# Attention and a gated feed-forward layer in one kernel: the first two heads in blocks of four key tiles, and query projections spread over the run

## The chip, the cores and the metric

The kernel runs on one core of one Trainium2 chip. The metric is the device time of one execution in microseconds (us), lower being better. A core has a matrix engine (TensorE, called PE in the profile, with PEld for its weight loads), a vector engine (VectorE, DVE), a scalar engine (ScalarE, ACT), a general engine (GpSimd, POOL) and SyncE (SP), which here only issues transfers. Sixteen DMA engines do the transfers. Each engine runs its own instructions in the order in which the program lists them.

## The reference

The input x has 2048 rows (tokens) of 512 numbers. One set of keys and values of width 16 serves all 32 heads; the feed-forward layer is 1792 wide; a gate g per token mixes the two.

```python
q = (x @ wq).reshape(B, S, H, Dh).transpose(0, 2, 1, 3)      # 32 heads of 16
k = x @ wk;  v = x @ wv                                      # one head of 16
p = softmax(einsum("bhqd,bkd->bhqk", q, k) * Dh ** -0.5)
a = einsum("bhqk,bkd->bhqd", p, v) ... @ wo
b = (silu(x @ w_gate) * (x @ w_up)) @ w_down
g = sigmoid((x * gate_w).sum(-1))
return g * a + (1 - g) * b
```

## The kernel before

All of it is one program with an order written out by hand. Numbers that need more than one rounded factor are held as a high part and a low part, so that a product takes three matmuls (`three`, line 111): high by high, high by low, low by high.

**The opening (lines 501 to 652).** x arrives, is transposed on TensorE and split. Keys and values are projected (`project_kv`). Then the queries of the first eight heads (m = 0) are projected for the four chunks c of 512 tokens, and `fill(GAP)` (line 652) does three more query projections whole. There are sixteen query projections: m = 0 to 3 (eight heads each) by c = 0 to 3. `query(m, c)` (line 214) makes one of them as a job of 12 matmuls; its inner function `keep` (line 224) empties the PSUM bank into a high part `qh`, a low part `ql` and a bound `qb` (the absolute value times the largest key, from which a head's score limit is had), takes a maximum, and stores the three parts to `q_d` in DRAM. For m = 0, head 0's rows go straight from these buffers into its tile `QS[0]` (line 244, sixteen small transfers), and the twelve stores to `q_d` come after all four chunks (line 650). For the other heads `load_head(h)` (line 660) reads four pieces from `q_d`, 64 and 192 KB in turn.

**The heads (lines 673 to 720).** A head is sixteen key tiles of 128 keys. For a tile, `score` (line 673) makes two pieces, one per pair of query chunks: two matmuls that use 64 rows of the array each and run beside one another, into one of two PSUM buffers `pss`. `exps` (line 687) takes the exponential on ScalarE, or, for some pieces, half from PSUM and half later from SBUF, where VectorE has copied it meanwhile (the copy of line 684). `mix` (line 692) multiplies a whole tile by the values: 8 records of line 700. At a head's end the sum is copied out (line 718) and divided in six pieces of VectorE work (`LATER`), the last of which stores the head to `o_d`.

**The feed-forward work** fills TensorE between the scores. `JOBS` (line 376) lists it: nine query projections that are left over, then for each chunk c the gate and up projections of 14 slices in groups of 5, 5 and 4, and behind each group the four `down` jobs of the group before. `feed(n)` takes n steps; in a step two jobs advance, one on the array's lower 64 rows and one on its upper 64 (`Halves`, line 394). When a job ends, its PSUM bank is emptied by VectorE at once (`EVAC`), except where a copy of a score is due next (`HOLD`). Work that can wait goes to the list `DEFER`, with a cost in us and a budget of 3.8 per block. Three PSUM banks `pf` serve the jobs. Weights come through two buffers `wraw`, are split on GpSimd (lines 107 and 108, through `load_split`), and in later chunks come back from DRAM ready split.

**The order of the heads.** The first two heads (32 tiles) go through the loop of lines 794 to 815, `BEGIN` = 16 turns of two tiles: four score pieces, four exponentials, all on ScalarE, 8 steps of `feed`, then `settle()`, which empties `DEFER`, and the two mixes. From tile 32 on `block` (line 731) does four tiles at a time: 8 score pieces and 16 steps in the order of `STEPS`, three of the eight pieces split between ScalarE and VectorE (`KINDS`, `EXPS`), then the deferred work and four mixes. The first such block (`TURN`) has ten score pieces. A block makes the scores of two tiles beyond those that it mixes. After the last block the jobs that are left run whole (`whole`, line 380) and `finish` multiplies the heads by wo.

**Memory.** `PT` holds six finished tiles, three in `bp` and three in a pool that is opened once the last query projection is done (`open_acc`, line 264), for until then the split x of chunks 2 and 3 and the split wq lie there. `ACC` holds sums of the feed-forward output.

Of the kernel before, what the change touches and what calls it, by code (L numbers as in the profile page):

```python
# [18 lines left out]
P = 128  # L19
S = 2048  # L20
D = 512
# [25 lines left out]
PTB = 3  # L47
WRB = 2
BLOCK = 4
BEGIN = 16  # L50
STOP = 2
EARLY = 6
OUTS = (1, 2, 3, 0)
# [3 lines left out]
TURN = "SS" + "SFF" * 8  # L57
# [5 lines left out]
def tile_gated_mix(ctx, tc, x, wq, wk, wv, wo, w_gate, w_up, w_down, gate_w, out):  # L63
# [10 lines left out]
    q_d = dpool.tile([H, 3 * DH, S], F32, name="q_d")  # L74
# [19 lines left out]

    qpool = tc.alloc_tile_pool(name="qpool", bufs=1, side="right")
# [7 lines left out]
    ACC, PAIR = {}, []  # L103
# [19 lines left out]
    ACTS, DEFER, LOADS, HOLD, EVAC, FRESH = [], [], [], [], [], set()  # L123
# [5 lines left out]
    def settle():  # L129
        FRESH.clear()  # L130
        run(ACTS, len(ACTS))
        while DEFER:
            DEFER.pop(0)[2]()
# [75 lines left out]
    WQ, QS, STORES = {}, {}, []  # L209

    def load_wq(m):
        WQ[m] = load_split(wq_v[:, :, m * P:(m + 1) * P], f"wq{m}", 1, qpool)

    def query(m, c):
# [8 lines left out]

        def keep(ps):
            qh = wp.tile([P, CH], F32R, name="hh", bufs=7)
            ql = wp.tile([P, CH], F32R, name="hl", bufs=7)

            if m:
                qb = wp.tile([P, CH], F32, name="ht" if c % 2 else "hs", bufs=2)
                nc.vector.tensor_copy(qh, ps)  # L230
            else:
                qb = wp.tile([P, CH], F32R, name="hl" if c % 2 else "hh", bufs=7).bitcast(F32)
                nc.scalar.activation(qh, ps, AF.Copy)
                nc.scalar.activation(qb.bitcast(F32R), ps, AF.Abs, scale=kmax)
            nc.vector.tensor_tensor(ql, ps, qh.bitcast(F32), ALU.subtract)
            if m:
                nc.vector.tensor_scalar(qb, qh.bitcast(F32), kmax, None, op0=ALU.mult)
                nc.vector.scalar_tensor_tensor(qb.bitcast(F32R), qb, -1.0, qb, op0=ALU.mult, op1=ALU.max)
            parts = [ql, qh, qb.bitcast(F32R)]
            if not m:  # L240
                for h, qs in QS.items():
                    for i, part in enumerate([qh] + parts):
                        row = c % 2 * RT + i * DH
                        nc.sync.dma_start(qs[row:row + DH, c // 2, :].bitcast(F32), part[h * DH:(h + 1) * DH].bitcast(F32))

            def store():
                for j, part in enumerate(parts):
                    nc.sync.dma_start(q_d[m * HG:(m + 1) * HG, j * DH:(j + 1) * DH, cs], part.bitcast(F32))

            if m:  # L250
                store()
            else:
                STORES.append(store)
            nc.vector.tensor_reduce(top[:, t:t + 1], qb, axis=AX.X, op=ALU.max)

        return Job(3 * KD, lambda: m in WQ, terms, keep)

    def queries():
        jobs = [query(m, c) for m in range(1, KD) for c in range(NCH)]
        jobs[-1].after.append(open_acc)  # L260
        jobs[-1].after.append(lambda: nc.vector.tensor_reduce(top[:, KD * NCH:], top[:, :KD * NCH], axis=AX.X, op=ALU.max))
        return jobs

    def open_acc():
        qpool.release()
        for name in ("accp", "bp2"):
            PAIR.append(tc.alloc_tile_pool(name=name, bufs=3, side="right"))
# [60 lines left out]
    def down(ns, c, i):  # L328
# [11 lines left out]
        def add(ps):  # L340
            if c not in ACC:
                ACC[c] = PAIR[0].tile([P, TC, D], F32, name="acc")
# [11 lines left out]


    def jobs():
        late = []
        for m, c in enumerate(ORDER):
            for fs in GROUPS:
# [7 lines left out]
                for j, job in enumerate(new):  # L367
                    yield job
                    if late and j:
                        yield late.pop(0)  # L370
                yield from late
# [129 lines left out]
    with tc.tile_pool(name="apool", bufs=1) as ap, tc.tile_pool(name="apool2", bufs=2) as a2:  # L501
# [29 lines left out]
        sel_i = ap.tile([P, HG], I32, name="sel_i")  # L531
        nc.gpsimd.iota(sel_i, pattern=[[-DH, HG]], base=0, channel_multiplier=1)
        sel_a = ap.tile([P, HG], F32, name="sel_a")
# [416 lines left out]
```

## Time and profile before

| | |
|---|---|
| median of three runs | 1343.21 us (1341.99 to 1344.04) |
| the profiled execution's own time | 1340.92 us |
| its span, first to last instruction | 1339.1 us |
| TensorE, busy | 1327.4 us, 99% |
| ScalarE, busy | 1069.0 us, 80% |
| VectorE, busy | 710.3 us, 53% |
| GpSimd, busy | 220.3 us, 16% |
| DMA, all queues | 151.84 MB |

The times of the table's lower part are of one profiled execution. A busy TensorE says little by itself, since its matmuls overlap: what counts is from one start to the next. A row of the view in order of time has the start, the length, the engine with the line, what is written and read, and how many instructions were merged; in brackets is the engine's idle time before it and what ended it. SPq rows are transfers as SyncE issues them; their length is the issue, not the transfer. In a table by windows a row has the stretch, its length, each engine's busy time with its count, the clock granted to TensorE as a share of full speed, the DMA engines' busy share and GB/s.

### The profile page before, as it was taken

Reading aid. Unit: us, or ns where it says so; the run is one execution under the profiler, and the core shown is the slowest. Engines: PE = TensorE matmul, PEld = TensorE weight load, DVE = VectorE, ACT = ScalarE, POOL = GpSimd, SP = SyncE. Lnnn points to the kernel's source line nnn. Section 1 sums busy time; section 2 is a strip of 40 time slices with the busy share of each in tenths; the row PEclk is TensorE's granted clock in tenths of the full one; section 3 lists DMA queues with packets and bytes.
Section 4 is the critical chain, followed back from the end, with each engine's and each line's share of the span. In section 5 each row is a group of like instructions: output and inputs, shape, how many; then the busy total and the mean of one; then the engine's idle time right before and its main releaser. Section 6 shows DMA issues by size and latency. Waiting matters only on the chain.

```text
span 1339.1 us, 26770 instructions
## 1 busy us (share of the span) xinstructions
PE 1327.4 (99%) x10743; PEld 769.7 (57%) x10743; DVE 710.3 (53%) x1221; ACT 1069.0 (80%) x1475; POOL 220.3 (16%) x228
## 2 busy tenths in 40 slices
PE   9999999999999999999999999999999999999998
PEld 7655555555555555555555555555555555555586
DVE  4555565465455555555555555455445565455442
ACT  4578888888888888888888888888888888888511
POOL 5141321152042141143020000000000000001223
PEclk9999999999999999999999999999999999999999
DMA  8455221131135372275162342243132342333154
GB/s 278 137 178 191 67 60 36 36 105 46 54 106 156 117 232 68 68 212 159 38 206 85 127 131 84 68 133 97 52 99 68 126 147 68 99 108 115 53 184 144
DMA packets 104178, 151.84 MB, mean 113 GB/s; under 512 B 12657, under 2 KB 43633, under 8 KB 102385
## 3 DMA queue, kind: packets, MB, share of 16 engines
q1 hardware_dynamic: 102320, 149.86, 36.4%
q8 instruction: 88, 1.44, 0.5%
q10 hardware_dynamic: 1728, 0.20, 0.1%
q14 instruction: 42, 0.34, 0.1%
HBM read 98.11 MB, written 51.38 MB: 112 GB/s over the span
## 4 chain that ended last, share of the span: by engine, by line
PE 98%; DVE 1%; ACT 1%; issue 0%; POOL 0%; DVEq 0%; ACTq 0%
PE pf L192 38%; PE po L700 34%; PE pss L680 21%; PE pf L117 4%; ACT pt L688 0%; PE pss L562 0%; PE po L549 0%; DVE xl L567 0%; PE pss L602 0%; DVE acc L345 0%; DVE hs L282 0%; POOL wul L108 0%; DVE wkv_l L108 0%; ACT xh L566 0%; DVE ot L464 0%
## 5 line engine op out<-in xcount | busy, mean ns | idle before, releaser
L688 ACT ACTIVATE pt<-pss 128x1024 f32<-128x1024 f32 (+1 forms) x1024 | 842.0, 876 | 177.7 <-PE pss L680 146.5
L684 DVE COPY pt<-pss 128x512 f32<-128x512 f32 x354 | 244.8, 691 | 421.4 <-PE pss L680 386.5
L700 PE MATMUL po<-pt,vaug 128*32 128x512 f32 x4096 | 467.6, 595 | 0.0
L680 PE MATMUL pss<-qs,ks 64*128 64x512 f32 x2048 | 402.4, 417 | 1.2 <-ACT pt L688 1.1
L680 PEld LDWEIGHTS pss<-qs,ks 64*128 64x128 f32 x2048 | 193.1, 184 | 218.7 <-ACT pt L688 183.5
L700 PEld LDWEIGHTS po<-pt,vaug 128*32 128x32 f32 x4096 | 119.2, 109 | 260.3 <-issue 255.2
L688 ACT ACTIVATE pt<-pt 128x512 f32<-128x512 f32 x354 | 195.7, 620 | 0.0
L192 PE MATMUL pf<-xh,wgl 64*128 64x512 f32 (+1 forms) x440 | 162.0, 391 | 0.0
L192 PE MATMUL pf<-xh,wgh 64*128 64x512 f32 (+1 forms) x440 | 160.8, 392 | 0.3
L192 PE MATMUL pf<-xl,wgh 64*128 64x512 f32 (+1 forms) x440 | 160.3, 390 | 0.0
L192 PE MATMUL pf<-xh,wuh 64*128 64x512 f32 (+1 forms) x440 | 158.3, 392 | 1.0 <-POOL wuh L107 0.5
L192 PE MATMUL pf<-xl,wuh 64*128 64x512 f32 (+1 forms) x440 | 158.1, 390 | 0.0
L192 PE MATMUL pf<-xh,wul 64*128 64x512 f32 (+1 forms) x440 | 157.1, 391 | 0.4 <-POOL wul L108 0.4
L192 PE MATMUL pf<-wdh,hl 64*128 64x512 f32 (+1 forms) x427 | 143.8, 390 | 0.0
L192 PE MATMUL pf<-wdh,hh 64*128 64x512 f32 (+1 forms) x427 | 143.3, 390 | 0.0
L192 PE MATMUL pf<-wdl,hh 64*128 64x512 f32 (+1 forms) x427 | 143.3, 390 | 0.0
L709 DVE RECIPROCAL rsb<-rsb 128x128 f32<-128x128 f32 x128 | 117.0, 935 | 10.1 <-issue 7.8
L447 POOL CAST xh<-wraw 128x512 fp32r<-128x512 f32 x4 | 2.9, 729 | 536.8 <-DMA wraw<-o_d 536.8
L192 PEld LDWEIGHTS pf<-xh,wgh 64*128 64x128 f32 (+1 forms) x440 | 78.5, 185 | 9.6 <-issue 1.3
L192 PEld LDWEIGHTS pf<-xh,wuh 64*128 64x128 f32 (+1 forms) x440 | 77.2, 185 | 9.7 <-issue 1.9
L192 PEld LDWEIGHTS pf<-xl,wgh 64*128 64x128 f32 (+1 forms) x440 | 78.5, 185 | 5.8
L192 PEld LDWEIGHTS pf<-xh,wgl 64*128 64x128 f32 (+1 forms) x440 | 78.5, 185 | 5.4
(158 smaller groups left out, 1361.5 us busy)
## 6 DMA issues: line engine op xcount, KB each, us to landing
qs<-q_d SPq DMA_DIRECT2D x62, 192.0 KB
wraw<-in_B_w_gate_dram SPq DMA_DIRECT2D x28, 256.0 KB
wraw<-in_B_w_up_dram SPq DMA_DIRECT2D x28, 256.0 KB
wraw<-in_B_w_down_dram SPq DMA_DIRECT2D x28, 256.0 KB
wgh<-w_d SPq DMA_DIRECT2D x28, 256.0 KB
wgl<-w_d SPq DMA_DIRECT2D x28, 256.0 KB
wuh<-w_d SPq DMA_DIRECT2D x28, 256.0 KB
wul<-w_d SPq DMA_DIRECT2D x28, 256.0 KB
```

What stands on the lines that cost most here:

```text
L117: nc.tensor.matmul(ps, a, b, start=(i == 0), stop=(i == n - 1))
L192: ins = nc.tensor.matmul(self.ps, a, b, start=(i == 0 and not half), stop=(last and half != 0))
L447: nc.gpsimd.tensor_copy(OT[c][0][:, k, :], raw)
L680: nc.tensor.matmul(ps[:, b * CH:(b + 1) * CH], ks[rows, kt * P:(kt + 1) * P], QS[h][rows, j, :], start=True, stop=True)
L684: other = nc.vector.tensor_copy(pt[:, CH:], ps[:, CH:]) if half else None
L688: ins = nc.scalar.activation(pt[:, w], ps[:, w], AF.Exp, scale=SCALE)
L700: nc.tensor.matmul(po[c * 2 * DH:(c + 1) * 2 * DH, :], vaug[:, kt, :], pt[:, c * CH:(c + 1) * CH], start=(kt == 0), stop=(kt == NT - 1))
L709: nc.vector.reciprocal(rsb[:, w], rsb[:, w])
```

## The change

The loop of two tiles goes; all 128 blocks of four tiles use the same order, after a short opening of two tiles (`OPEN`: four score pieces, eight steps). For this the room must be free from the start, so:

- x's chunks 2 and 3 and wq leave their pool before the first head. The split wq lies in two of the three `ACC` buffers (`HOME`), the projected keys and values in the third.
- Only five query projections stay ahead of the feed-forward work: three whole in `fill(GAP)` (`EARLY_Q`) and two first in `JOBS` (`SECOND_Q`). The other seven (`LATE`) are placed one in each group of gate and up projections, behind its fifth job. Their `qh` and `ql` lie in `hp`, one of them in a buffer `osb`.
- For `SECOND_Q` and `LATE` the scaling, the bound and the maximum of `qb` go to `DEFER`; those of `LATE` through a list `SOON`, and a third pass over `DEFER` takes query work last.
- For the others, ScalarE makes `qh` and `qb`, as it did for m = 0 alone.
- `q_d` has the layout of a head's tile: per head 128 rows of two chunks. A projection stores four pieces (`qh` twice). wq's columns are permuted (`by_row`), so that a store's slowest dimension has 16 places, where it had 8 before. A head comes as one transfer of 256 KB, head 0 too, which now goes to `q_d` and back.
- The first gate and up weights are asked for ahead of `fill(GAP)`.

```diff
-PTB = 3
+PTB = 6
-BEGIN = 16
+EARLY_Q = ((1, 2), (1, 3), (2, 3))
+SECOND_Q = ((1, 0), (1, 1))
+LATE = {(0, 0): (2, 0), (0, 1): (3, 0), (0, 2): (2, 1), (1, 0): (3, 1), (1, 1): (2, 2), (1, 2): (3, 2), (2, 0): (3, 3)}
-TURN = "SS" + "SFF" * 8
+OPEN = "SFSFFFSFFFSF"
...
-    q_d = dpool.tile([H, 3 * DH, S], F32, name="q_d")
+    q_d = dpool.tile([H, P, 2, CH], F32, name="q_d")
...
+        late = (m, c) in LATE.values()
+        behind = late or (m, c) in SECOND_Q
         def keep(ps):
...
+            if behind:
                 nc.vector.tensor_copy(qh, ps)
             else:
                 nc.scalar.activation(qh, ps, AF.Copy)
                 nc.scalar.activation(qb.bitcast(F32R), ps, AF.Abs, scale=kmax)
             nc.vector.tensor_tensor(ql, ps, qh.bitcast(F32), ALU.subtract)
...
+            def store(js=range(3)):
+                for i, j in enumerate((1, 0, 1, 2)):
+                    if j in js:
+                        row = c % 2 * RT + i * DH
+                        nc.sync.dma_start(q_d[m * HG:(m + 1) * HG, row:row + DH, c // 2, :].rearrange("h r s -> r h s"),
+                                          parts[j].bitcast(F32))
...
+            if behind:
+                store([0, 1])
+                (SOON if late else DEFER).extend([((m, c), 0.5, scale), ((m, c), 0.7, bound), ((m, c), 0.7, most)])
+            else:
                 store()
+                most()
...
+                    if j == 4:
+                        if (m, GROUPS.index(fs)) in last:
+                            yield last[m, GROUPS.index(fs)]
...
-            run(STORES, NCH)
             load_wq(3)
+            nc.sync.dma_start(new_qs(0).bitcast(F32), q_d[0])
+            for nm in "gu":
+                load_w(nm, 0)
             fill(GAP)
+    qpool.release()
...
         def load_head(h):
...
+            nc.sync.dma_start(new_qs(h).bitcast(F32), q_d[h])
...
-            for last in (False, True):
+            for stage in range(3):
...
-                    if n in kept or (n in FRESH) != last or cost > left:
+                    if n in kept or (2 if isinstance(n, tuple) else n in FRESH) != stage or cost > left:
...
-            for j in range(2):
-                exps(*score(0, j))
-            for n in range(BEGIN):
...
-            for k in range(2 * BEGIN // BLOCK, NB):
+            tiles = [(u, j) for u in range(2) for j in range(2)]
+            for what in OPEN:
+                if what == "S":
+                    exps(*score(*tiles.pop(0)))
+                else:
+                    feed(1)
+            for k in range(NB):
```

145 lines of the change are left out of this document (58 added, 87 removed).

## The prediction

> **What bounds the kernel now.** I read the page first, then the chain of work that ended last in order of time, and then the waits and the order of time of single stages.
>
> ```profile
> span 1339.1 us, 26770 instructions
> PE 1327.4 (99%) x10743; PEld 769.7 (57%) x10743; DVE 710.3 (53%) x1221; ACT 1069.0 (80%) x1475; POOL 220.3 (16%) x228
> ...
> PE 98%; DVE 1%; ACT 1%; issue 0%; POOL 0%; DVEq 0%; ACTq 0%
> ```
>
> The chain lies on TensorE for 98% of the span. So an edit counts only if TensorE finishes its list sooner: fewer stops between scores, steps and mixes. The change leaves the number of matmuls as it is. What it moves is seen in the chain from the first score on:
>
> ```profile
> 48.59 0.67 PE pss L680 x4
> ...
> 54.02 1.85 PE po L700 x16
> ...
> 127.18 1.86 PE po L700 x16
> 138.02 2.26 PE po L700 x17
> ```
>
> Each row with L700 is the start of a turn's mix. First score 48.59, first mix 54.02, sixteenth 127.18: fifteen turns of two tiles in 73.16, or 4.88 each, 9.75 for four tiles. The block that follows takes 10.84. The later blocks are had from one window that runs from that block's mix to a late one, with line 700's records counted, and the row of that late mix:
>
> ```profile
> 137.95:1243.64 1105.69, 425.92 (x3745) 109.67 (x3745) 1.00 0.34 101
> ```
>
> ```profile
> 1243.64 0.64 PE L700 MATMUL po<-pt,vaug 128*32 128x512 f32 x4
> ```
>
> 32 records make a block, so 3745 are 117 blocks: 1105.69 / 117 = **9.45 for four tiles**, stalls included. A turn of two tiles thus loses 0.15 against half a block. The waits up to 130 us say where:
>
> ```profile
> PEld pss L680 <- ACT pt L688: 17.0, 32, 0.8
> ```
>
> Two waits per turn, about 0.5 us each, for an exponential that has not freed its score buffer. (They stand on the weight load, and part is hidden under running matmuls.)
>
> **The change part by part.**
>
> *The first two heads as blocks.* A normal block, the next one, which had late weights, and the first exponentials:
>
> ```profile
> 585.76 4.76 ACT L688 ACTIVATE pt<-pss 128x1024 f32<-128x1024 f32 x6 [0.70 <-PE pss L680]
> ...
> 591.37 3.64 PE L700 MATMUL po<-pt,vaug 128*32 128x512 f32 x32
> ...
> 597.57 0.57 SPq L665 DMA_DIRECT2D qs<-q_d  x1
> ...
> 599.26 0.50 PE L192 MATMUL pf<-xh,wuh 64*128 64x512 f32 x1 [0.48 <-POOL wuh L107]
> ```
>
> ```profile
> 602.21 3.64 PE L700 MATMUL po<-pt,vaug 128*32 128x512 f32 x32
> ```
>
> ```profile
> 49.22 1.94 ACT L688 ACTIVATE pt<-pss 128x1024 f32<-128x1024 f32 x2 [7.57 <-issue]
> ```
>
> The opening has no mix for ScalarE to catch up under, so ScalarE sets it. From the first score to its exponential 0.63 (48.59 to 49.22); four whole exponentials at 1.94 / 2 = 0.97 make 3.88; the six of a block before its mix take 4.76; from their end to the mix 0.85 (590.52 to 591.37). Sum 10.1 to the first mix of a block, of tiles 0 to 3. TensorE's own part is shorter: 12 score pieces and 24 steps at about 0.23 make 8.3. The mix of the ninth block (tiles 32 to 35) follows 8 x 9.45 = 75.6 later, at 85.7 from the first score. Before, that same mix came 138.02 - 48.59 = 89.4 after it. **Gain 3.7.**
>
> *Eight steps more.* Up to that mix the old order did 16 x 8 + 16 = 144 steps, the new one does 8 + 9 x 16 = 152. The jobs' work is the same, so eight steps leave the end:
>
> ```profile
> 1263.70 25.43 PE pf L192 x111
> ```
>
> Here 111 whole matmuls run after the heads at 0.229 each. Eight of them are **1.8 of gain**; by whole jobs it may be 12 of them, with some steps more in the last two blocks.
>
> *Head 0's queries go to DRAM and back.* Before, the last operation of m = 0's projections, the first and a late transfer into `QS[0]` and the stores to `q_d` look so:
>
> ```profile
> 41.68 0.69 DVE L235 TENSOR_TENSOR hl<-pf,hh 128x512 fp32r<-128x512 f32 x1 [1.44 <-ACT hl L234]
> ```
>
> ```profile
> 32.10 0.63 SPq L244 DMA_DIRECT2D qs<-hh  x1
> ...
> 42.40 0.51 SPq L244 DMA_DIRECT2D qs<-hl  x1
> ...
> 45.05 1.29 SPq L248 DMA_DIRECT2D q_d<-hh  x2
> ```
>
> ```profile
> 54.77 1.25 SPq L248 DMA_DIRECT2D q_d<-hl  x1
> ```
>
> ```profile
> 20.00:22.00 2.00, 2.00 (x19) 1.94 (x18) 0.67 (x1) 1.85 (x3) 1.41 (x3) 1.00 1.05 430
> ...
> 50.00:52.00 2.00, 2.00 (x11) 1.39 (x10) 1.90 (x4) 2.00 (x4) 0.00 (x0) 1.00 0.50 189
> ```
>
> The first stores of `q_d` cost SyncE 0.65 each; once the DMA queues are full, 1.25, and then the sixteen DMA engines are half busy at 189 GB/s, while the store of x to DRAM at 20 us kept them all busy at 430. The old store, whose slowest dimension is 8 heads, seems held to half of the engines; the new one has 16 rows there. I take 0.65 per store, so four keep up with a projection (2.7 us). The last `ql` is ready at 42.37, and three stores follow on SyncE: 42.40 + 3 x 0.65 = 44.35. What a store with a load behind it takes is seen at the kernel's end, where a head goes to `o_d` and its rows come back:
>
> ```profile
> 1276.34 1.73 SPq L714 DMA_DIRECT2D o_d<-osb  x4
> ```
>
> ```profile
> 1282.45 0.61 POOL L447 CAST xh<-wraw 128x512 fp32r<-128x512 f32 x1 [12.28 <-DMA wraw<-o_d]
> ```
>
> From the first store's issue to the use 6.1, from the last one's end 4.4. So the first score can come between 44.35 + 4.4 = 48.7 and 43.7 + 6.1 = 49.8, where it came at 48.59: a loss of 0.1 to 1.2. I take **0.8**, nearer the upper end, since wq's last quarter is fetched just ahead of it. What hid the transfers so far are the three projections of `fill(GAP)`, which end at 48.5; beyond them nothing covers. Head 0's sixteen small transfers and the twelve late stores go, and this costs or gains nothing by itself.
>
> [...]
>
> Behind the wait for head 0's stores stand on SyncE the first gate and up weights, the twelve stores of the three whole projections and head 1's load. At 0.65 each they are issued by about 57. Who waits for them: block 1 for the weights and the seven `hh` buffers for the stores, both after 60, and block 3 for head 1.
>
> *Late queries on VectorE.* A projection's five operations, first and last (the second is line 235's, above):
>
> ```profile
> 43.19 0.69 DVE L230 CAST hh<-pf 128x512 fp32r<-128x512 f32 x1 [0.23 <-PE pf L192]
> ...
> 45.76 0.69 DVE L254 TENSOR_REDUCE top<-hs 128x1 f32<-128x512 f32 x1
> ```
>
> ```profile
> L684 DVE COPY pt<-pss 128x512 f32<-128x512 f32 x354 | 244.8, 691 | 421.4 <-PE pss L680 386.5
> ```
>
> 3.3 in all (43.19 to 46.45), of which 1.4 at once and 1.9 deferred. Nine projections (two `SECOND_Q`, seven `LATE`) now do this inside blocks where VectorE also copies three score halves. VectorE is busy 53% of the span, so a block of 9.45 has 4.4 free; the deferred part lies under the mix of 3.64. The 1.4 at once can hold up a copy (0.69 in the group's row) by up to 0.7, and with it a score buffer. That can happen only while a step's end falls in the first three of a block's sixteen steps: behind these the next copy is close, and `HOLD` puts the emptying after it from the fourth on. 9 x 3/16 x 0.7 is 1.2; I take **1.0**, with 0 and 9 x 0.7 = 6.3 as ends. A late `ql` also takes one of the two buffers `osb`, so the next head's copy waits until the head before has landed in `o_d`. That store is the last deferred piece of a head and the copy comes about 6 us later (3.64 of mix and five score pieces), where the store at the kernel's end took 6.1 to its use, load included; I take 0.
>
> *The weights.* The feed-forward work starts some 50 us earlier, after 24 steps instead of 108. Its first weights are asked for behind head 0's rows, at about 47, and are needed in block 1, after 60. A head's load falls from four issues of about 0.6 to one. The block before 602.21 took 602.21 - 591.37 = 10.84, 1.39 over the mean, for a weight whose issue came late in a crowded queue. The new order may lose that stall or put it elsewhere; I take 0, with -1.4 and +2.8 (two such) as ends.
>
> *Free of cost:* the smaller preparation of `sel`, the maximum of `top` at the end (VectorE waits there for TensorE), and the permuted splits of wq:
>
> ```profile
> 36.07 1.29 POOL L108 TENSOR_TENSOR wq2l<-wraw,wq2h 128x512 fp32r<-128x512 f32 x1
> ```
>
> wq2 is ready at 37.4 and wanted by the third whole projection, 12 matmuls before 48.5, at 45.8. The two splits ahead would have to grow from 3.8 to over 12 us before TensorE waits.
>
> **Sum:** -3.7 - 1.8 + 0.8 + 1.0 = **-3.7**, against the profiled execution's 1340.92. That execution was 2.3 under the median 1343.21; I take the difference over to the median: **1339.5**.
>
> **The rivals.**
>
> *Stores at the old pace (slower).* If sixteen engines don't share the new stores, sixteen stores at 1.25 from 32.1 on (where the first part is ready; four follow per projection) end at 52.1, and the last one's start is 50.9; with 6.1 more the first score comes at 57.0, 8.4 late in place of 0.8. 1339.5 + 7.6 = 1347.1. It decides once the first score is later than 48.6 + 4.5 = 53.1. For it speaks the crowded queue: 4 MB to move in 12 us. Against it the 430 GB/s of the x store. [...]
>
> *VectorE in the way (slower).* If each of the nine projections costs a block its whole 1.4, that is 12.6 in place of 1.0: 1351. For no change 0.5 each is enough. For it: VectorE feeds the score buffers, and one late copy stops TensorE. Against it: the free half, and that thirteen of sixteen places in a block leave the next copy alone.
>
> *The gain is given back by late weights (same).* Two more stalls like that of 602 take 2.8: 1342.3. For it: the early weights stand in SyncE's queue behind the return of head 0, and GpSimd splits them one after another.
>
> *Better than that.* The start loses nothing, the stall of 602 goes, twelve matmuls leave the end: -3.7 - 2.7 - 1.4 = -7.8: 1335.4.
>
> **How the numbers follow.** Forecast 1339.5 with its own range 1336 to 1341.5: chance 0.46. Better: 0.13. Late weights: 0.18. VectorE: 0.14. Old pace: 0.09. About 0.2% of the time, 2.7, is what a measurement here can tell from no change, so faster means under 1340.5 and slower over 1345.9. Faster: 0.13 + most of the forecast + a little of the weights = 0.58; slower: 0.09 + most of the VectorE case = 0.20; same: 0.22. The range goes from 1335 to 1347, which leaves out the worse half of the two slow cases and a little below.
>
> **What would show it.** First score at about 49.4; the first mix ten us later and the ninth mix near 135; the mixes 9.45 apart from the start. Stores of `q_d` at 0.65 on SyncE, and a DMA share near 1 between 33 and 45. About 100 whole matmuls after the heads. Blocks with a late projection at most 0.7 longer than others. It would be wrong if the first score comes after 53, if waits of scores on VectorE's copies add up to more than 5, or if a new row of TensorE waiting for GpSimd's splits appears in the first 200 us.

## The result, and the profile after

The changed kernel takes 1349.01 us (median of six, 1348.22 to 1349.76) beside 1342.60 (1341.58 to 1344.04) on the same chip: a ratio of **1.0047 (95% interval 1.0034 to 1.0060)**, slower. The prediction said 1339.5, and its range ended at 1347. The profiled execution took 1348.94, its span is 1347.0. From the profile page of the changed kernel, its span, TensorE's busy time and the granted clock in 40 slices:

```profile
span 1347.0 us, 26709 instructions
...
PE 1328.4 (99%) x10743; PEld 767.6 (57%) x10743; DVE 722.0 (54%) x1237; ACT 1076.9 (80%) x1508; POOL 221.4 (16%) x227
...
PEclk9799999999999999999999999999999999999999
```

There are as many matmuls as before, and 7.9 us more of span. The second slice (34 to 67 us) has the digit 7, a mean clock of 0.80, where the kernel before had full clock. TensorE's own waits, by total, number and longest:

```profile
PE pss L698 <- DMA qs<-q_d: 4.5, 1, 4.5
PE pf L198 <- DVE sign L446: 1.8, 2, 1.6
PE pss L698 <- DVE sign L446: 1.6, 1, 1.6
```

The first is the wait for head 0's queries; the other two rows hold two stops of 1.6, at 276 and 474 us. In order of time, on SyncE's queue and on TensorE (start, duration):

```profile
44.69 1.20 SPq L265 DMA_DIRECT2D q_d<-hl  x1
...
49.16 0.35 SPq L672 DMA_DIRECT2D qs<-q_d  x1
```

```profile
52.67 0.56 PE L698 MATMUL pss<-qs,ks 64*128 64x512 f32 x2 [4.52 <-DMA qs<-q_d]
...
67.76 1.06 PE L718 MATMUL po<-pt,vaug 128*32 128x512 f32 x8
```

The last store of m = 0 to `q_d` is issued at 44.69 and has landed at 48.98; only then is head 0's load issued, which lands at 52.53. The first score comes at 52.67 (before 48.52), and the first mix another 15.1 us later, not 10.1. What lies between is seen in a table by stretches of 3.41 us: length, busy time and count of TensorE, weight load, VectorE, ScalarE and GpSimd, then the granted clock, the DMA share and GB/s.

```profile
46.15:49.56 3.41, 2.00 (x9) 1.31 (x7) 1.40 (x3) 1.72 (x3) 0.00 (x0) 1.00 0.83 249
49.56:52.98 3.42, 0.31 (x3) 0.34 (x5) 1.17 (x2) 0.00 (x0) 2.55 (x2) 1.00 0.74 230
52.98:56.39 3.41, 3.41 (x14) 2.67 (x11) 0.00 (x0) 2.57 (x3) 2.72 (x4) 0.50 0.75 234
56.39:59.80 3.41, 3.14 (x10) 2.02 (x9) 0.39 (x1) 2.73 (x4) 1.05 (x1) 0.50 0.96 305
59.80:63.22 3.42, 3.42 (x12) 2.72 (x13) 1.05 (x3) 1.19 (x3) 0.00 (x0) 0.50 1.00 319
63.22:66.63 3.41, 3.41 (x18) 2.62 (x18) 0.69 (x1) 2.04 (x3) 0.00 (x0) 0.50 1.00 286
66.63:70.04 3.41, 3.41 (x32) 1.46 (x34) 0.06 (x1) 3.41 (x6) 0.82 (x2) 1.00 0.57 170
```

Behind the nearly empty stretch the clock is 0.50 for **four stretches, 13.65 us**, and TensorE, which was not to be the bound here, is busy for 0.92 or more of each. The blocks behind are as forecast: from the first mix to the ninth 75.9 (143.66 - 67.76; forecast 75.6). The same window as before, from the ninth mix to a late one, and the matmuls of jobs behind the heads:

```profile
143.66:1250.76 1107.10, 425.93 (x3744) 109.67 (x3744) 1.00 0.33 105
```

```profile
1270.30:1347.00 76.70, 25.50 (x111) 20.76 (x111) 0.98 0.51 164
```

1107.10 where it was 1105.69, and 111 whole matmuls as before. So the 7.9 are: first score +4.15; first score to ninth mix +1.6 (91.00 against 89.43: 3.4 gained, 5.0 lost); the blocks +1.4; from the last block's mix to the end +0.7 (79.1 to 79.8).

### The profile page after: what moved, and what is told of

Read it like the earlier page. It is cut to its first block, busy times and chain, and to the rows that moved or that the text cites. A ratio compares the mean times of both kernels' runs of the same rounds, so it can differ in the third digit from the quotient of the medians.

```text
span 1347.0 us, 26709 instructions
## 1 busy us (share of the span) xinstructions
PE 1328.4 (99%) x10743; PEld 767.6 (57%) x10743; DVE 722.0 (54%) x1237; ACT 1076.9 (80%) x1508; POOL 221.4 (16%) x227
## 5 line engine op out<-in xcount | busy, mean ns | idle before, releaser
L706 ACT ACTIVATE pt<-pss 128x1024 f32<-128x1024 f32 (+1 forms) x1024 | 833.0, 864 | 172.8 <-PE pss L698 146.4
L702 DVE COPY pt<-pss 128x512 f32<-128x512 f32 x381 | 263.5, 692 | 449.9 <-PE pss L698 413.8
L706 ACT ACTIVATE pt<-pt 128x512 f32<-128x512 f32 x381 | 210.5, 620 | 0.0
L198 PE MATMUL pf<-xh,wuh 64*128 64x512 f32 (+1 forms) x440 | 161.0, 392 | 0.1
L198 PE MATMUL pf<-xh,wul 64*128 64x512 f32 (+1 forms) x440 | 160.2, 392 | 0.0
L198 PEld LDWEIGHTS pf<-xl,wgh 64*128 64x128 f32 (+1 forms) x440 | 79.8, 185 | 5.7
L198 PEld LDWEIGHTS pf<-xh,wgl 64*128 64x128 f32 (+1 forms) x440 | 79.8, 185 | 5.6
```

The source lines that it names most:

```text
L198: ins = nc.tensor.matmul(self.ps, a, b, start=(i == 0 and not half), stop=(last and half != 0))
L702: other = nc.vector.tensor_copy(pt[:, CH:], ps[:, CH:]) if half else None
L706: ins = nc.scalar.activation(pt[:, w], ps[:, w], AF.Exp, scale=SCALE)
```

## The experiments

All are the changed kernel with the edits given. Ratios are to the kernel before, measured on the same chip; times in us from the profiled execution. "Half clock" is the time at 0.50 before the ninth mix. A ratio rests on 5 to 11 executions, the other times on one.

| run | ratio (95%) | first score | first mix | half clock | ninth mix |
|---|---|---|---|---|---|
| before | 1 | 48.52 | 53.95 (two tiles) | 0 | 137.95 |
| changed | 1.0047 (1.0034 to 1.0060) | 52.67 | 67.76 | 13.65 | 143.66 |
| again | 1.0054 (1.0040 to 1.0068) | 52.09 | 67.17 | 13.65 | 143.14 |
| keep_warm | 1.0015 (1.0006 to 1.0024) | 53.05 | 66.06 | 6.83 | 142.02 |
| keep_warm4 | 1.0028 (1.0016 to 1.0041) | 55.32 | 67.36 | 3.41 (at 13.5 us) | 143.60 |
| direct | 1.0049 (1.0033 to 1.0066) | 47.88 | 63.57 | 10.24 | 141.40 |
| direct_c0 | 1.0010 (1.0001 to 1.0019) | 47.99 | 61.56 | 6.83 | 138.80 |
| own_first | 1.0057 (1.0043 to 1.0071) | 49.10 | 64.18 | 6.83 | 142.33 |
| gap60 | 1.0157 (1.0144 to 1.0170) | 53.85 | 68.94 | 10.24 | 155.13 |
| late_less | 1.0040 (1.0026 to 1.0053) | 52.02 | 67.11 | 13.65 | 143.45 |
| wide_open | 1.0079 (1.0065 to 1.0093) | 48.62 | 59.89 | 6.83 | 144.05 |
| wide_open2 | 1.0068 (1.0055 to 1.0082) | 48.26 | 59.54 | 6.83 | 143.20 |
| direct_warm | 1.0035 (1.0023 to 1.0048) | 47.59 | 59.66 | 3.41 | 140.64 |
| direct_thin | 1.0052 (1.0039 to 1.0066) | 47.82 | 64.36 | 10.24 | 141.20 |
| direct_warm_b | 1.0031 (1.0019 to 1.0043) | 47.72 | 59.79 | 0 | 139.54 |
| direct_warm_d | 1.0021 (1.0012 to 1.0030) | 47.82 | 59.90 | 0 | 138.33 |
| gates_first | 1.0011 (1.0002 to 1.0020) | 47.93 | 59.99 | 0 | 136.29 |
| gates_first_f | **0.9988 (0.9979 to 0.9997)** | 48.18 | 59.56 | 0 | 136.00 |

### The wait, the opening and the clock: keep_warm, direct, own_first, gap60

My theory was two losses at the start, the late first score and the clock that falls because of it. The rivals were an opening that is slow in itself, and a loss in the blocks.

**keep_warm** fills the wait:

```diff
             fill(GAP)
+            pad = ps_f.tile([P, CH], F32, name="pf")
+            for _ in range(18):
+                nc.tensor.matmul(pad, WQ[1][0][:, 0], XC[2][0][:, 0], start=True, stop=True)
```

> Eighteen throwaway matmuls (128x128 by 512 columns, about 0.23 us each by the rows of the changed kernel) stand on TensorE right behind the last whole projection, so that the 4.5 us of waiting for head 0's queries are filled; the wait itself stays, and nothing else is changed. Theory (two losses at the start: the wait, and a clock that falls to 0.5 for 13.65 us because of it): granted clock 1.00 throughout, first score still near 52.7, first mix 10.1 us behind it in place of 15.1, and the time 1349.0 - 5.0 = 1344.0. Rival A (the opening is slow because ScalarE, the transfers or the gate weights are late): first mix still 15 us behind the first score, and 1349. Rival B (the loss lies in the blocks, in late query work on VectorE): 1349 as well, though the clock stays up.

The ratio fell from 1.0047 to 1.0015, about as expected. One of eleven executions, the profiled one, had a mean clock of 0.996 and took 1346.27; the other ten had 0.999 or 1.000 and took 1342.78 to 1344.36. In the profiled one the clock fell all the same, later, in the opening. Two stretches of it:

```profile
54.13:57.55 3.42, 2.84 (x15) 1.00 0.94 276
57.55:60.96 3.41, 3.41 (x12) 0.50 0.98 313
```

TensorE was busy 0.83 of the stretch before the fall, and had waited 0.2 for head 0's queries, in place of 4.5: here the clock fell without that wait.

**direct** sends head 0's rows straight from SBUF into its tile:

```diff
+            else:
+                for i, j in enumerate((1, 0, 1, 2)):
+                    row = c % 2 * RT + i * DH
+                    nc.sync.dma_start(QS[0][row:row + DH, c // 2, :].bitcast(F32), parts[j].rearrange("(r h) s -> h r s", h=HG)[0].bitcast(F32))
+                STORES.append(store)
...
+            run(STORES, NCH)
             load_wq(3)
-            nc.sync.dma_start(new_qs(0).bitcast(F32), q_d[0])
```

> Head 0's rows go straight from the buffers in SBUF into its query tile, four small transfers per projection, and the sixteen stores for all heads follow them once the four projections are issued; all else as in the changed kernel. Theory: first score back at 48.5 (the kernel before has 48.5), no idle window on TensorE and no fall of the clock, first mix near 58.6; of the 9.1 us the whole is saved: 1349.0 - 9.1 = 1339.9. Rival A (the opening is slow for another reason): the first score gains 4 us, the opening stays 15 us long, 1345. Rival B (loss in the blocks): the start gains, but the later weights and stores take it back; 1346 to 1349.

The first score came at 47.88, and the first mix still 15.7 behind it; no gain in all (1.0049). The stores now came last and held the buffers `hh`; ScalarE's queue and the score that waits for it:

```profile
48.49 1.02 ACT L713 ACTIVATE pt<-pss 128x1024 f32<-128x1024 f32 x1 [4.77 <-issue]
49.41 0.59 ACT L257 ACTIVATE hh<-pf 128x512 fp32r<-128x512 f32 x1
...
51.50 4.45 ACT L713 ACTIVATE pt<-pss 128x1024 f32<-128x1024 f32 x5
```

```profile
52.61 0.80 PE L705 MATMUL pss<-qs,ks 64*128 64x512 f32 x2 [1.85 <-ACT pt L713]
```

Two whole projections are emptied between the first and the second exponential. So this run undid one wait and made another, and it showed that the opening can lower the clock without any wait for head 0.

**own_first** keeps the way through DRAM, but with four 32 KB stores per projection for head 0 alone; the sixteen of 256 KB follow the load:

```diff
+                    nc.sync.dma_start(q_0[row:row + DH, c // 2, :], parts[j].rearrange("(r h) s -> h r s", h=HG)[0].bitcast(F32))
...
+            nc.sync.dma_start(new_qs(0).bitcast(F32), q_0)
+            run(STORES, NCH)
             load_wq(3)
```

> Head 0 still goes through DRAM, but alone and ahead: four stores of 16 rows (32 KB) per projection into a place of their own and one load; the sixteen stores for all heads (256 KB each) follow the load. Theory 1 (the round trip came late because 4.2 MB stand ahead of it in the transfer engines, at 320 GB/s): first score at 48.2 to 50, the wait under 2 us, no fall of the clock, time 1340 to 1341.5. Theory 2 (a store and a load that depends on it cost about 8 us whatever the load): the last small store is issued near 43.5, first score near 51.5, wait 3.3; whether the clock then falls isn't known: 1343 without, 1348 with.

First score 49.10, a wait of 1.1: theory 1. The stores and head 0's load by size and median time to their landing, and one stretch with its DMA share and GB/s, of own_first and then of the changed kernel:

```profile
32.00:46.00 14.00, 14.00 (x64) 11.59 (x63) 9.03 (x14) 5.11 (x11) 5.97 (x5) 1.00 0.14 39
```

```profile
qs<-q SPq DMA_DIRECT2D x1, 512.0 KB, 3.5
q<-hh SPq DMA_DIRECT2D x10, 32.0 KB, 1.8
```

```profile
32.00:46.00 14.00, 14.00 (x64) 11.58 (x63) 9.04 (x14) 5.79 (x12) 6.18 (x5) 1.00 0.82 256
```

```profile
q_d<-hl SPq DMA_DIRECT2D x7, 256.0 KB, 3.8
qs<-q_d SPq DMA_DIRECT2D x1, 512.0 KB, 3.4
```

So 3.6 of the 4.15 (52.67 - 49.10) come from the way of the stores, and 0.6 are left for the round trip as such. Of the 3.6 the last store's issue is 1.2 (43.46 in own_first, 44.69) and its landing 2.5 (1.8 behind the issue, 4.3); the load takes as long in both. The run changes the size of the stores and the crowd ahead at once. What the size alone does is seen where the late projections store 256 KB, with less in the engines (the blocks' DMA share is 0.33):

```profile
q_d<-qh SPq DMA_DIRECT2D x21, 256.0 KB, 3.0
```

By that row some 1.2 of the 2.5 would be the size and 1.3 the 4.2 MB ahead, an estimate. The clock and the total were not theory 1's: the late stores hold `hh` as in direct, a score waits 2.5 for ScalarE until 55.6, the clock falls there, and the ratio is 1.0057.

**gap60** (`GAP = 60`) does two more projections whole under the wait.

> GAP = 60 in place of 36: the two projections SECOND_Q run whole in the gap, under the wait for head 0, and no longer in blocks. Theory: TensorE is busy to about 53.6, no idle window, clock 1.00; first score at 53.6 to 54, first mix 10.1 later at 63.9 (3.9 earlier than in the changed kernel); two whole jobs fewer are left after the heads (7 in place of 9), 2 x 12 to 15 x 0.23 = 5.5 to 6.9 there: 1349.0 - 3.9 - 6 = 1339. Rival A (opening slow for another reason): first mix at 68.7, 1344. Rival B: the two projections on VectorE cost in the blocks what is saved by their leaving: 1338 or less.

The worst of all, 1.0157, against every theory. A score waits 2.9 for a copy on VectorE at 63.7; and with `SECOND_Q` gone from the blocks the first gate and up weights are wanted at once, and GpSimd has not split them:

```profile
76.17 0.50 PE L198 MATMUL pf<-xh,wgh 64*128 64x512 f32 x1 [2.93 <-POOL wgh L111]
...
93.08 0.50 PE L198 MATMUL pf<-xh,wgh 64*128 64x512 f32 x1 [2.54 <-POOL wgh L111]
```

The ninth mix came 11.5 later than in the changed kernel. In the changed kernel, which has no such wait, the steps of `SECOND_Q` stand ahead of these weights.

### Work by rows in a window: keep_warm4, direct_c0, wide_open, direct_warm, direct_thin

The stretches of half clock have lengths of 3.41 us or a multiple of it (6.83, 10.24 and 13.65 in the table). I added up the matmuls that start in each such window, each by the part of the 128x128 array that it uses; fifteen whole ones, at the 0.229 each of the prediction, fill a window. A lone 64-row step counts half.

**keep_warm4** adds two throwaways behind each of the opening's four scores; **direct_c0** is direct with the first projection's stores issued at once (`if c == 0: run(STORES, 1)`); **wide_open** adds to that the first gate and up loads ahead of the stores and an opening of full-height matmuls:

```diff
-OPEN = "SFSFFFSFFFSF"
+OPEN = "SFFFSFFFSFFFSFFF"
...
-                    feed(1)
+                    if not now:
+                        now.extend([JOBS.pop(0), 0])
+                    now[0].step(now[1])
+                    now[1] += 1
```

> The eighteen throwaway matmuls as before, and two more full-height ones (128 rows, 512 columns) behind each of the four scores of the opening, where TensorE waits for ScalarE's exponentials anyway. In the runs so far the clock fell whenever the matmuls that start within one window of 3.41 us came to 0.43 of the work of fifteen full-height ones or less, a 64-row matmul counted as half, and stayed whole at 0.46 and more; it was not the share of busy time that decided (0.83 busy fell, 0.70 busy stayed). Theory (work by rows in a window): with these eight the opening's windows come to 0.6 and more, the clock stays 1.00 throughout, and the first mix comes 10 to 11 us behind the first score in place of 13.0: 1343.4 - 2.5 = 1341. Rival (the opening is slow in itself, by ScalarE's exponentials): the clock may stay, but the first mix is 13 us behind, 1343.5 or, with TensorE now more loaded, 1345.

> Head 0 straight in SBUF as before, but the first projection's four stores for all heads are issued at once, between its rows and those of the second, so that the buffers hh and hl come free before the whole projections want them; in the run before they came free at 49, and ScalarE evacuated two projections (2.1 us) between the first and the second exponential while TensorE waited 1.85. Theory: that wait goes, ScalarE evacuates before 48.7, first score at 48.5. Whether the clock falls is decided by the opening's own lone 64-row steps, 0.43 to 0.5 of a full window's work: if it stays, first mix at 58.6 and 1340.5; if one window falls, 6.8 us at half, first mix at 61.5, 1343.5. Rival (the clock falls only behind an idle stretch of 2 us or more): it stays, 1340.5.

> As the kernel before it in this list, and the opening's eight 64-row steps are replaced by twelve full-height matmuls of one more whole projection (1,0); the first gate and up weights are asked for ahead of the remaining stores. Theory (work by rows in a window): 12 full steps and 8 half ones over 4.5 us, 0.75 and more, the clock stays 1.00; first score at 48.5, first mix at 58.8 to 59.5 (8.5 earlier than in the changed kernel); one whole job fewer behind the heads, 2.7 to 3.4: 1349.0 - 8.5 - 3 = 1337.5. Rival (the first weights become late, as in GAP = 60, where TensorE waited 2.9 twice and 2.5 once for GpSimd's splits): one to three waits of 1 to 3 us in the first four blocks, each with a fall of the clock, 1341 to 1347.

keep_warm4 kept its clock through the whole opening, 12.0 from score to mix; by 0.229 each, 1.8 of it are the eight throwaways. It is no faster than keep_warm. Its first score comes 2.6 later than the changed kernel's, but the profiled execution is the slowest of six: in it TensorE waited 2.7 for a split of x up to 12.86, and the clock was 0.50 from 13.5 to 16.9. direct_c0 lost the 1.85 of direct, had one window of 0.33 work (49.39 to 52.80) and then 6.83 of half clock: the second branch of its expectation, 1.0010. That is 5 us less than the changed kernel, by head 0's way and the order of the stores alone. The half clock itself cost little in the total here: five executions with a mean clock of 0.999 took 1341.94 to 1343.07, four with 0.997 took 1342.42 to 1344.07. wide_open kept the clock in the opening (11.3), but then TensorE waited 4.1 up to 92.36 for the split of a gate weight, and the clock fell there; it missed its 1337.5 by far (1.0079).

**direct_warm** is direct_c0 with the two throwaways per score; **direct_thin** differs in their rows alone:

```diff
-                        nc.tensor.matmul(pad, WQ[1][0][:, 0], XC[0][0][:, 0], start=True, stop=True)
+                        nc.tensor.matmul(pad, WQ[1][0][:2 * DH, 0], XC[0][0][:2 * DH, 0], start=True, stop=True)
```

> Head 0 straight in SBUF with the first projection's stores early, as in the run that came to 1.001 of the kernel before, and two throwaway full-height matmuls behind each of the opening's four scores. Theory (the half clock is set by the work of a 3.41 us window, and the opening's lone 64-row steps give too little): the window that held 0.33 of a full one's work gets 0.5 or more, the clock stays 1.00, the first mix comes 10.5 to 12 us behind the first score in place of 13.6, 1342.9 - 2.3 = 1340.6 (1339.5 to 1341.3), ratio about 0.9995. Rival (the opening is bound by ScalarE, the clock costs nothing there): the clock stays and the first mix is 13.6 behind, 1343.

> As the kernel with head 0 straight in SBUF and two throwaway matmuls behind each of the opening's scores, but these have 32 rows in place of 128: as many instructions of the same 512 columns and the same time, a quarter of the rows. Theory (work by rows in a window of 3.41 us decides the clock): the window that had 0.60 falls to 0.33 to 0.42, the clock falls to 0.5 for 6.8 us as without throwaways, first mix 13.6 to 14.5 behind the first score, and the later weights are in time, so the total is 1343 to 1344.5. Rival (time in which TensorE is busy, or the number of matmuls, decides): the clock stays 1.00 as with 128 rows, first mix 12.1 behind.

The throwaways by shape in the first window of the opening (busy, mean ns), and the windows (TensorE's busy time and count, clock, DMA share, GB/s); first direct_warm, then direct_thin:

```profile
L826 PE MATMUL pf<-xh,acc 128*128 128x512 f32 x6 | 2.2, 448 | 0.0
```

```profile
48.27:51.69 3.42, 3.42 (x14) 1.00 0.94 293
51.69:55.10 3.41, 3.41 (x16) 1.00 1.00 330
```

```profile
L826 PE MATMUL pf<-xh,acc 32*128 32x512 f32 x6 | 2.3, 458 | 0.0
```

```profile
48.43:51.84 3.41, 3.41 (x14) 1.00 0.95 303
51.84:55.25 3.41, 3.41 (x11) 0.50 1.01 346
55.25:58.67 3.42, 3.42 (x13) 0.50 0.84 235
58.67:62.08 3.41, 3.41 (x14) 0.50 0.48 162
```

Fourteen matmuls and a TensorE busy all the time in both, work 0.60 against 0.35: with 32 rows the clock falls, and the first mix comes 16.5 behind the first score, with 128 rows 12.1. **At the same busy time, the rows decided.** The two runs are of different chips, but all 22 executions of direct_warm_d and gates_first, which have the 128-row throwaways too, show a mean clock of 0.999 or more, and the five of direct_thin 0.998 or less. Over the 18 traces, from 25 to 1325 us, fifteen windows at full clock were followed by half: fourteen had 0.35 or less, one 0.43. Of 6,804 followed by full clock none had less than 0.33, and three less than 0.40; busy shares went down to 0.54 there. Of the half windows, the 18 that stayed half had 0.40 or less, with TensorE busy 0.74 to 1.00; of the fifteen behind which full clock came back twelve had 0.40 or more, and three, with mixes in them, 0.27 to 0.33. So there is no sharp border: between 0.33 and 0.43 windows stand on both sides, and the border between 0.43 and 0.46 in the expectation of keep_warm4 does not hold (in the changed kernel a window of 0.40 at 274.84 kept the clock). Ahead of 25 us, where x is transposed, this count does not fit: seventeen windows with 0.22 to 0.37 kept the clock, and one with 0.10, in keep_warm4, lost it. A transpose of 128 columns there starts every 0.11 us (sixteen in 1.91 at 19.95 in the kernel before), twice its share by columns (0.229 / 4), so the count may be too low. By this count the changed kernel stayed half so long because many of the opening's 64-row matmuls run alone: the first three of its four windows at half clock have a work of 0.27 to 0.37, the fourth, behind which the clock came back, 0.53.

direct_thin had 3.4 more of half clock than I expected, and took longer in all (1.0052). direct_warm did about what it should in the opening (12.1; 10.5 to 12 expected) and missed in the total, 1.0035 where 0.9995 was expected. The next part says why.

### Weights and late queries: late_less, direct_warm_b, wide_open2, direct_warm_d, gates_first, gates_first_f

**late_less** leaves out L272 and L276 for the seven `LATE` projections (`if not late:` ahead of each; `top` is cleared first); **direct_warm_b** sets their costs:

```diff
-((m, c), 0.5, scale), ((m, c), 0.7, bound), ((m, c), 0.7, most)
+((m, c), 0.5, scale), ((m, c), 1.8, bound), ((m, c), 1.0, most)
```

> As the changed kernel, but the seven projections done inside blocks leave out the magnitude (L272) and the maximum (L276) of their bound on VectorE; that part of the bound is not computed. Theory (deferred VectorE work of a late projection spills past the mix and, slowed by GpSimd's split, holds up the score copies): the two TensorE stalls of 1.6 us at 276 and 474 go, the stretch from the ninth mix to the last falls from 1123.5 by 1.5 to 3, nothing changes before 70 us: 1346 to 1347.5. Rival (the stalls come from the order of the jobs and the weights alone): same two stalls, 1348.5 to 1349.5.

> The kernel before it in this list, with the planner's costs of the late projections' bound set from 0.7 to 1.8 and of its maximum from 0.7 to 1.0, so that they are put off to a mix with room for them. Theory (late VectorE work that spills past the mix made the TensorE stall of 1.6 in the block at 466): that stall goes, 1.5 less than the kernel before it. Rival (the stall follows the phase of the jobs): it stays, or comes up in another block; same time within 0.7.

In the changed kernel, the bound of a late projection, GpSimd's split beside it, the score copies behind it, and TensorE:

```profile
471.25 1.78 DVE L272 SCALAR_TENSOR_TENSOR qh<-qh 128x512 fp32r<-128x512 f32 x1
...
472.94 1.29 DVE L702 COPY pt<-pss 128x512 f32<-128x512 f32 x2
```

```profile
470.86 1.62 POOL L112 TENSOR_TENSOR wul<-wraw,wuh 128x512 fp32r<-128x512 f32 x1
```

```profile
473.77 0.50 PE L698 MATMUL pss<-qs,ks 64*128 64x512 f32 x2 [1.58 <-DVE sign L446]
```

The bound took 1.78, at the median of the seven 0.69. With it left out, or put off by its cost, the stop in this block is gone in both runs. The other one, at 276.37, stayed in both, 1.6, so it isn't the late queries. There, in the changed kernel, it is a step of the feed-forward work on VectorE that takes 1.39 in place of 0.69, beside a split of GpSimd again:

```profile
274.11 1.39 DVE L321 SCALAR_TENSOR_TENSOR ht<-ht,hs 128x512 f32<-128x512 f32 x1
```

```profile
273.65 1.30 POOL L112 TENSOR_TENSOR wul<-wraw,wuh 128x512 fp32r<-128x512 f32 x1
```

```profile
276.37 0.46 PE L198 MATMUL pf<-xh,wgh 64*128 64x512 f32 x1 [1.59 <-DVE sign L446]
```

late_less gained 0.6 in the window of blocks, less than its theory; direct_warm_b's blocks took 1.6 less than direct_warm's (1106.0, 1107.6), but its total only 0.0004 of the ratio, inside the intervals.

**wide_open2** and **direct_warm_d** are wide_open and direct_warm with the first group's five down weights queued in `LOADS` (direct_warm_d also has the first gate and up loads ahead of the stores); **gates_first** queues them only when the first gate job ends:

```diff
-        for n in GROUPS[0]:
-            load_w("d", n)
+        first_gate.after.append(lambda: LOADS.extend([lambda n=n: load_w("d", n) for n in GROUPS[0]]))
```

**gates_first_f** is gates_first with one throwaway per score and direct_warm_b's costs.

> The opening with twelve full-height matmuls of a whole projection, as before, and the five down weights of the first group in the queue behind jobs, so that the third gate weight isn't behind them. Theory: the wait of 4.1 at 92 us for GpSimd's split and the two half-clock stretches behind it go, the fourth block falls from 15.5 to 10; the rest as in the run before, where the blocks from the ninth mix to the end took 3 to 4 more than in the changed kernel: 1352.8 - 6 = 1347. Rival (the splits of five down weights merely come later): the wait moves to the next blocks, 1350 or more.

> The first of this list, with the first gate and up weights asked for ahead of the stores, and the five down weights of the first group in the queue behind jobs instead of at once. Theory (the first four blocks last 10.0 each because of late weights): they fall to 9.45 to 9.6, 1.5 less than the first of this list. Rival (they are long because GpSimd's splits slow VectorE's operations and the second queries lie there): no change within 0.7.

> Head 0 straight in SBUF, two full-height throwaways behind each opening score, first gate and up weights ahead of the stores; the five down weights of the first group are queued only when the first gate job ends, so that the third gate weight is fetched and split ahead of them. Theory (an earlier start makes the third gate weight late, because two raw buffers and GpSimd take five down weights first): the waits of 0.53 and 0.63 at 94 to 96 go, the fifth block falls from 11.1 to 9.5 to 9.9, time 1344.5 - 1.4 = 1343, ratio 1.001. Rival (the wait goes on to the next weights): the block stays at 11 or the next one grows, 1344.5.

> The kernel before it in this list with one throwaway per opening score in place of two, and with the planner's costs of the late bound at 1.8 and 1.0. Theory: the throwaway left out saves 0.5 to 0.9 if the clock still stays at 1.00 (work of the thinnest window 0.47), and the stall in the block at 460 goes (1.5): ratio 0.9995, about the time of the kernel before. Rival: with one throwaway the clock falls again (6.8 us at half), 1344.

> The changed kernel as it is, beside the others on the same chip: 1.0047 of the kernel before, first score 52 to 52.7, clock 0.5 for 13.65 us from 53.

What direct_warm won, it lost at 95.77: TensorE and GpSimd there, then GpSimd in gates_first.

```profile
95.77 0.56 PE L198 MATMUL pf<-xh,wgh 64*128 64x512 f32 x2 [1.76 <-POOL wgh L111]
```

```profile
95.10 0.61 POOL L111 CAST wgh<-wraw 128x512 fp32r<-128x512 f32 x1 [2.25 <-DMA wraw<-in_B_w_gate_dram]
```

```profile
82.49 0.67 POOL L111 CAST wgh<-wraw 128x512 fp32r<-128x512 f32 x1 [4.80 <-DMA wraw<-in_B_w_gate_dram]
```

The third gate weight stood behind five down weights. Ahead of them it is split 12.6 us sooner; the waits go, and the fifth block falls from 13.3 (direct_warm) and 11.1 (direct_warm_d) to 9.4. wide_open2 still waited 3.0 there and missed its 1347. direct_warm_d missed: its first blocks stayed at 10.05, 9.93 and 9.80, which speaks for the rival; that its time fell by the 1.5 expected (1.7) is luck, by the fifth block. gates_first gave the block and 1.0011, as expected, and gates_first_f **0.9988, below the changed kernel and, by a little, the one before** (the interval ends at 0.9997). Its span, clock and opening:

```profile
span 1336.7 us, 26748 instructions
...
PEclk9999999999999999999999999999999999999999
```

```profile
48.18 0.50 PE L708 MATMUL pss<-qs,ks 64*128 64x512 f32 x2
...
59.56 0.64 PE L728 MATMUL po<-pt,vaug 128*32 128x512 f32 x4
```

## Why the prediction was wrong, step by step

**The step that failed is "Head 0's queries go to DRAM and back", at +0.8.** The first score lost 4.15 and, through the clock, 5.0 more. The pace of the stores was nearly right (0.55 to 0.65 for most, up to 1.2 at the end; the engines were 0.82 busy at 256 GB/s). What was wrong is the price of the way behind the last store. I took 4.4 to 6.1 from the kernel's end, where a store has 32 KB and the load behind it 256 KB. Here they have 256 and 512 KB (a head's load is 512 KB, not the 256 KB given under the change), behind 4.2 MB of other stores: the last store landed after 4.3 and the load after another 3.4, and the issue came 1.0 later: 44.69 to 52.53, 7.8. own_first, with the same way and 32 KB stores, had its first score at 49.10, inside the 48.7 to 49.8 of the prediction.

Two readings behind the 0.65 were my estimates: that an issue took 1.25 because the queues were full, and that the old store kept half of the engines because its slowest dimension has 8 places. The rows of before show 1.23 to 1.58 an issue from 46 to 58 us, with the engines 0.49 to 0.53 busy at 129 to 205 GB/s; with the new stores the changed kernel's rows show 0.82 at 256 GB/s (32 to 46 us) and 1.00 at 319 (59.80 to 63.22). No run changes the number of places alone.

By the profiled spans the forecast was 3.7 under 1339.1, and 1347.0 is 11.6 more. Of these the first score is 3.4 (4.15 in place of 0.8), the stretch from it to the ninth mix 5.3 (+1.6 in place of -3.7), the eight steps 1.8, the blocks 0.4 and the end 0.7.

**The clock** was no term of the sum. direct_warm and direct_thin were busy alike in the first window of the opening (3.42 and 3.41, 14 matmuls each); behind it one had 1.00 and the other 0.50, and 4.4 us of opening lie between them (12.1, 16.5), though both carry throwaways. In the changed kernel it is 15.1 against 10.1 forecast, or about 10.5 by gates_first_f (11.4 less 0.9 for four throwaways), an estimate. Busy time did not tell when the clock would fall or come back: direct_thin's fell behind a window busy all the time, and three windows in the changed kernel, busy 0.92 or more, were each followed by another at half clock.

**The first two heads as blocks, -3.7:** the blocks were sized rightly (75.9 against 75.6 from first to ninth mix), the 10.1 of the opening held only at full clock. With the clock kept, gates_first_f gains 1.6 from first score to ninth mix (87.8 against 89.4), not 3.7: 0.9 are its throwaways, and the second and third block take 10.06 and 10.09 in place of 9.45.

**Eight steps more, -1.8:** nothing, because the steps were miscounted. The first turn of the old order does 16 steps, not the 8 that the section on the order of the heads has for every turn: lines 798 and 801 feed 8 more. So the old order had done 16 + 15 x 8 + 16 = 152 steps up to that mix, as many as the new one. The traces agree: 287 half-height matmuls of jobs start before it in the kernel before and 286 in the changed one, and 111 whole ones follow the heads in both.

**Late queries on VectorE, +1.0:** measured +1.4 in the blocks, near by luck. The part that I priced, the 1.4 at once, is not what stopped TensorE. The deferred part, which I put under the mix for nothing, is what spilled out in one of the two stops, made longer beside GpSimd; the other stop has no late query in it. No run here took the split away. In the kernel before and the changed one 16 of 116 such operations (bounds and silu steps, 128x512) ran beside a two-input split of GpSimd and took 0.78 to 1.78; of the 100 others none took more than 0.69. Over the 18 traces 133 of 1,016 took more than 0.9, and each of the 133 ran beside such a split.

**The weights, 0:** true of the changed kernel (no wait for GpSimd from 55 to 200 us), but by luck, it seems, since the start was 9 us late. Once the start was mended in direct_warm, the third gate weight became the bound, as the rival of late weights had it, at another weight than I named. **The end, +0.7** after the last mix, is scatter of single executions: `again`, the same kernel, has 78.9 there, and the kernel before 79.1.

The rival "Stores at the old pace" gave 1347.1 with a first score at 57.0; it came nearer in time than the forecast, by a mechanism that wasn't there. The last store was issued 1.0 later than I had it, not 7.2 (50.9 against 43.7); the rest of the delay is the landing of a store and a load that are both larger than those I took the price from, with the bulk ahead of them.

## What to carry to other kernels

Price a round trip through DRAM at the sizes and under the load that it will have, not from smaller transfers at another place (7.8 here from the last store's issue to the load's landing, where I had priced 4.4 to 6.1), and let the small part that the next stage needs go ahead of the bulk (own_first: first score at 49.10 in place of 52.67). Where TensorE runs half-height steps alone, count work by rows as well as busy time: here the openings' windows of 0.33 (direct_c0) and 0.35 (direct_thin) were followed by a clock of 0.50, and with two full-height throwaways per score (direct_warm, 0.60) it stayed at 1.00 there. Count steps in the program's own loops, first turns included. Whoever mends a late start should look at once for what it had been hiding: here the weights behind it.

## What the runs showed of the hardware

I had not expected the clock to fall, from 1.00 to 0.50, behind a window in which TensorE was busy throughout (direct_thin, 48.43 to 51.84, work 0.35), nor to stay at 0.50 for four windows (changed kernel, 13.65 us) in which TensorE was busy 0.92 or more. In the changed kernel a 128x512 bound on VectorE took 1.78 (at 471.25) in place of 0.69, and a silu step 1.39 (at 274.11) in place of 0.69, while GpSimd's two-input split ran. Its sixteen stores of 256 KB behind one another landed 2.9 to 4.3 us after their issue, the last ones latest, with the engines 0.82 busy; own_first's 32 KB stores of head 0's rows, with the engines 0.14 busy, landed after 1.8.
